# The second feed-forward's second layer as seven block products for eight, with a transposed output and a written task order

## The chip, the cores and the metric

The kernel runs on one core of one Trainium2 chip. The metric is device time of one execution in microseconds (us); smaller is better. Engines are named as the profile names them: PE (TensorE matmul), PEld (its weight load), DVE (VectorE), ACT (ScalarE), POOL (GpSimd), SP (SyncE, which here issues DMA transfers).

## What is computed

Masked attention over 4 batches and 8 heads (576 tokens, head size 64), then a gated feed-forward (512 to 1536 to 512), then a second feed-forward (512 to 2048 to 512) whose nonlinearity is h·cos(h). The change concerns the last lines.

```python
x = attention(q, k, v, tau)          # (4*576, 512), heads put side by side
gate = sigmoid(x @ w_gate)           # (2304, 1536)
x = (gate * (x @ w_val)) @ w_out     # (2304, 512)
h = x @ w_in                         # second feed-forward, first layer: (2304, 2048)
out = (h * cos(h)) @ w_out2          # second feed-forward, second layer: (2304, 512)
```

Every matmul operand is held as two parts of reduced precision ("hi" and "lo", lo being the operand minus hi), and one product is three matmuls: hi·hi, hi·lo, lo·hi.

## The kernel before

The 2304 tokens are handled as four blocks of 512 (the first 512 of each batch) and one small block of 256 (the last 64 of each batch). A class `Plan` (line 142) collects tasks, each with an engine, a cost and a due time, and `put_out` issues them: at each step the engine whose next task can begin first gets it, and among the tasks that can begin the one with the smallest due time goes first. Each engine then runs its tasks in exactly the order so fixed. For the attention (first `put_out`, line 919) the kinds of the tasks stand in a written list, `ORDER`; for everything behind it (second `put_out`, line 1453) the due times alone decide.

Behind the attention come two stages. In the **gated stage** (about 400 to 740 us) the first feed-forward runs; beside it `stage_weights` (line 991) reads the two 64-bit weight matrices of the second feed-forward, rounds them, splits them into hi and lo and stores them to a DRAM tensor `wd`: per slice of 256 columns the weights "i" (first layer), "s" (sums and differences of quarters of "i") and "z" (second layer). The lo parts are made on POOL (L987), the sums on DVE (L1019).

In the **second stage** (about 740 us to the end) the blocks go in two passes of two blocks, (0,1) and (2,3). For each of 8 slices of 256 hidden columns `quad` (line 1279) computes the first layer of both blocks at once as a 2x2 block product with seven block products instead of eight (42 matmuls for 48); its partial results are copied between PSUM banks by ACT (L1267) and added by DVE (L1270). Its inputs are seven "forms" of the activations (`forms_of`, line 1229). Then `cosine` works on each of four results: ACT scales to an integer (L1328), DVE removes the period in two steps (L1329 reads PSUM, L1331 reads SBUF alone), ACT takes the absolute value and the sine (L1333, L1334), DVE multiplies by h, which stands in PSUM (L1133), ACT takes the hi part (L1094), DVE the lo part (L1097). `second_c` (line 1343) is the second layer: per block, slice and half slice, four groups of 128 tokens as the stationary operand against 512 columns of "z", three matmuls each (L1360 to L1362); after every one or two slices the four PSUM banks are added by DVE to a running sum (L1370; the first time copied by ACT, L1368). That is 24 matmuls per block and slice, 384 for the two blocks of a pass. The small block runs in the first pass only (`U` its first layer, `S` its second). Weight slices of 1 MB come from `wd` by SP's queue into a ring of six (`fetch`, line 1421): three per slice and pass.

Of the kernel before, what the change touches and what calls it, by code (L numbers as in the profile page):

```python
# [19 lines left out]
P = 128  # L20
# [8 lines left out]
SM = 512  # L29
# [70 lines left out]

SHARED = (
# [19 lines left out]


# [19 lines left out]
class Plan:  # L142
# [31 lines left out]
    def task(self, engine, cost, key, fn, *needs, uses=(), moved=0.0, alone=False):  # L174
# [8 lines left out]
        return t  # L183

# [116 lines left out]
def tile_kernel(ctx: ExitStack, tc: tile.TileContext, q, k, v, tau, w_gate, w_val, w_out, w_in2, w_out2, out):  # L301
# [13 lines left out]
    minus_r = const.tile([P, P], F32R, tag="minus_r", name="minus_r")  # L315
    nc.vector.tensor_scalar(minus_r, ident, -1.0, None, op0=ALU.mult)
# [100 lines left out]
    at = tctx.enter_context(tc.tile_pool(name="at", bufs=1, side="right"))  # L417
    ps_s = psA.enter_context(tc.tile_pool(name="ps_s", bufs=2, space=PSUM))
# [509 lines left out]
    po = ctx.enter_context(tc.tile_pool(name="po", bufs=4, space=PSUM))  # L928
# [16 lines left out]
    END = len(items)  # L945

# [26 lines left out]

    for kd, ft in [("o", ft) for ft in range(NA)] + [(kd, ft) for ft in range(NA, NB) for kd in "gvo"]:
# [3 lines left out]
        loaded[kd, ft] = piece(plan, tmp, 2, kd, ft, wts[kd, ft], lambda i: first_use - 14.0 + i)  # L978

    wd = dpool.tile([P, NC, 3, 2, 1024], F32, name="wd")  # L980
    in_dram = {}

    def staged(key, hi, lo, needs, uses, to):
# [3 lines left out]
        last = task("POOL", 1.225, key, lambda: nc.gpsimd.tensor_tensor(st()[:, 1], lo(), f32(st()[:, 0]), op=ALU.subtract),  # L987
                    last, uses=[st, *uses])
        return task("SP", 0.47, key, lambda: nc.sync.dma_start(to, f32(st())), last, uses=[st], moved=1024)

    def stage_weights(ft, keys):

        done = {"i": [], "s": [], "z": []}
        ts = []
        for kd in "iz":
            for x, last, t in words(plan, tmp, 2, kd, ft, None, lambda i: next(keys)):
                i = x.i
                done[kd].append(staged(x.key, lambda x=x: f32(x.t), lambda x=x: f32(x.t), [last], [t],
                                       wd[:, ft, 0 if kd == "i" else 2, :, SM * i:SM * i + SM]))
                ts.append((x, last, t))  # L1000
            if kd == "i":
                (x0, l0, b0), (x1_, l1, b1) = ts
                key = next(keys)
                sf = ring("sf", [P, 4, 2, P], F32, 1)

                def quarter(x, f):
                    return f32(x.t).rearrange("p (c f n) -> p c f n", c=2, f=2)[:, :, f]

                def form(k):
                    return sf()[:, k]  # L1010
# [498 lines left out]
```

## Time and profile before

| | |
|---|---|
| median of 3 runs | 1134.39 us (1133.38 to 1135.61) |
| profiled execution, its own time | 1132.12 us |
| span of its profile, first to last instruction | 1130.0 us |
| PE busy | 1106.1 us (98%) |
| DVE / ACT / POOL busy | 875.2 (77%) / 730.4 (65%) / 408.9 us (36%) |
| granted TensorE clock, mean | 0.998 of full |

A matmul's row lasts longer than the distance to the next one, since matmuls are pipelined; the cost of one more or one less is the distance from start to start. The same holds, by a little, for DVE and ACT.

### The profile page before, as it was taken

The page shows a single profiled execution, that of the slowest core. Times are in us where ns is not written, and L with a number is a line of the kernel's source. Part 1 is how long each engine was busy: PE and PEld are TensorE (multiplying, and loading weights), DVE is VectorE, ACT ScalarE, POOL GpSimd, SP SyncE. Part 2 cuts the span into 40 slices and gives each one's busy share as a digit, 9 for nine tenths or more (in the row PEclk, how much of TensorE's full clock was granted, in tenths as well). Part 3 has the DMA queues.
Part 4 walks back from the last instruction along what each step waited for, and adds up shares of the span by engine and source line. Part 5 has one row for each costly group of instructions (what it writes and reads, how often), then busy time and mean ns, then how long its engine had stood idle before and what let it go on. Part 6 is the DMA issues. An engine that isn't in the chain of part 4 may idle for free. (4 is left out here: it accounts for less than half of the span.)

```text
span 1130.0 us, 17172 instructions
## 1 busy us (share of the span) xinstructions
PE 1106.1 (98%) x6031; PEld 950.5 (84%) x6031; DVE 875.2 (77%) x1620; ACT 730.4 (65%) x1409; POOL 408.9 (36%) x336
## 2 busy tenths in 40 slices
PE   7989999999999999999999999999999999999998
PEld 6878888888888888988888888878888888888887
DVE  6999989999998866787326889988576777857674
ACT  6889988897888855655314555477664645666461
POOL 3787788776778333451003555340000000000000
PEclk9999999999999999999999999999999999999999
DMA  6444544543244266595003988994343333735322
GB/s 172 137 122 150 149 135 119 183 136 94 74 132 152 82 229 217 168 359 178 22 1 105 338 319 317 350 321 151 112 142 106 125 112 116 275 122 182 143 75 75
DMA packets 64101, 183.57 MB, mean 162 GB/s; under 512 B 8336, under 2 KB 8592, under 8 KB 56080
## 3 DMA queue, kind: packets, MB, share of 16 engines
q1 hardware_dynamic: 63856, 182.15, 48.1%
q8 instruction: 48, 0.79, 0.3%
q10 hardware_dynamic: 160, 0.33, 0.1%
q14 instruction: 37, 0.30, 0.1%
HBM read 131.07 MB, written 51.38 MB: 161 GB/s over the span
## 5 line engine op out<-in xcount | busy, mean ns | idle before, releaser
L723 DVE SCALAR_TENSOR_TENSOR p<-s,sm,p 128x576 f32<-128x576 f32 x128 | 102.9, 813 | 9.6 <-ACT p L720 4.1
L715 DVE TENSOR_REDUCE sm<-s 128x1 f32<-128x576 f32 x144 | 105.6, 751 | 5.6 <-PE s L709 4.2
L1094 ACT ACTIVATE g<-g 128x512 fp32r<-128x512 f32 x118 | 74.0, 629 | 53.7 <-DVE g L1133 51.9
L1097 DVE TENSOR_TENSOR g<-g,g 128x512 fp32r<-128x512 f32 x118 | 94.9, 810 | 17.4 <-ACT g L1094 16.3
L1125 PE MATMUL h<-x,w 128*128 128x256 f32 (+1 forms) x304 | 101.3, 333 | 0.0
L1126 PE MATMUL h<-x,w 128*128 128x256 f32 (+1 forms) x304 | 101.3, 333 | 0.0
L1124 PE MATMUL h<-x,w 128*128 128x256 f32 (+1 forms) x304 | 101.3, 333 | 0.0
L1360 PE MATMUL o<-w,g 128*128 128x512 f32 x256 | 99.8, 390 | 0.0
L1361 PE MATMUL o<-w,g 128*128 128x512 f32 x256 | 99.7, 389 | 0.0
L1362 PE MATMUL o<-w,g 128*128 128x512 f32 x256 | 99.6, 389 | 0.0
L720 ACT ACTIVATE p<-s,sm 128x576 f32<-128x576 f32 x128 | 93.8, 747 | 8.6 <-DVE sm L715 5.3
L709 PE MATMUL s<-kk,qh 128*128 128x288 f32 x320 | 95.8, 318 | 1.3 <-DVE p L723 0.5
L686 POOL TENSOR_TENSOR PT<-praw,PT 128x512 fp32r<-128x512 f32 x60 | 78.3, 1306 | 48.6 <-ACT praw L681 24.4
L666 ACT ACTIVATE PT<-t 128x512 fp32r<-128x512 f32 (+1 forms) x160 | 85.9, 557 | 11.6 <-PE t L739 10.2
L709 PE MATMUL s<-kk,ql 128*128 128x288 f32 x320 | 88.9, 296 | 0.5 <-DVE ql L516 0.5
L368 POOL TENSOR_TENSOR w<-wt,w 128x512 fp32r<-128x512 f32 x30 | 41.2, 1381 | 126.9 <-ACT w L364 126.5
L739 PE MATMUL t<-ident,p 128*128 128x128 f32 x512 | 76.3, 274 | 4.9 <-DVE PT L677 1.9
L352 ACT ACTIVATE we<-wraw 128x512 f32<-128x512 f32 x68 | 45.6, 673 | 47.8 <-DMA wraw<-in_moe_w_out_dram 21.0
L1298 PE MATMUL h<-form,w 128*128 128x512 f32 x192 | 75.2, 392 | 1.1 <-ACT h L1267 1.0
L1300 PE MATMUL h<-form,w 128*128 128x512 f32 x192 | 74.7, 389 | 0.0
L1299 PE MATMUL h<-form,w 128*128 128x512 f32 x192 | 74.7, 389 | 0.0
L739 PEld LDWEIGHTS t<-ident,p 128*128 128x128 f32 x512 | 60.2, 140 | 15.1 <-DVE LT L677 3.0
(191 smaller groups left out, 3358.5 us busy)
## 6 DMA issues: line engine op xcount, KB each, us to landing
w<-wd SPq DMA_DIRECT2D x48, 1024.0 KB, 4.8
wd<-stage SPq DMA_DIRECT2D x48, 512.0 KB, 4.6
gd<-st SPq DMA_DIRECT2D x64, 256.0 KB, 3.6
wraw<-in_moe_w_out_dram SPq DMA_DIRECT2D x28, 512.0 KB, 5.2
raw_k<-in_k_dram SPq DMA_DIRECT2D x30, 304.0 KB, 4.7
raw_q<-in_q_dram SPq DMA_DIRECT2D x30, 288.0 KB, 4.5
wraw<-in_moe_w_in_dram SPq DMA_DIRECT2D x16, 512.0 KB, 5.3
early<-gd SPq DMA_DIRECT2D x7, 1024.0 KB, 6.5
```

What stands on the lines that cost most here:

```text
L709: nc.tensor.matmul(s[:, half, 0:HALF], qq[:, off:off + P], kk[:, k0:k0 + HALF], start=(i == 0), stop=(i == len(mms) - 1),)
L715: nc.vector.tensor_reduce(self.sm()[:, 0:1], self.s()[:, :, 0:HALF], axis=AX.XY, op=ALU.min)
L720: nc.scalar.activation(self.e, self.s()[:, :, 0:HALF], AF.Exp, bias=self.sm()[:, 0:1], scale=-1.0)
L723: nc.vector.scalar_tensor_tensor(self.e, self.s()[:, :, 0:HALF], self.sm()[:, 1:2], self.e, op0=ALU.is_le, op1=ALU.mult, accum_out=self.su ...
L739: nc.tensor.matmul(tp[:, c * P:(c + 1) * P], self.pn[:, k0:k0 + P], ident, is_transpose=True, start=(c == 0), stop=(c == 3))
L1097: nc.vector.tensor_tensor(g()[:, 1, 0:n], g32()[:, 0:n], f32(g()[:, 0, 0:n]), op=ALU.subtract)
L1124: nc.tensor.matmul(o, w_hi, x(0, c), start=begin, stop=False, **late)
L1125: nc.tensor.matmul(o, w_hi, x(1, c), start=False, stop=False, **late)
L1126: nc.tensor.matmul(o, w_lo, x(0, c), start=False, stop=c == KC - 1, **late)
L1360: nc.tensor.matmul(o(), hi, w_hi, start=i == 0, stop=False)
L1361: nc.tensor.matmul(o(), hi, w_lo, start=False, stop=False)
L1362: nc.tensor.matmul(o(), lo, w_hi, start=False, stop=i == len(parts) - 1)
```

## The change

The second layer of the two blocks of a pass is computed for slices 0 to 6 as a 2x2 block product with seven products for eight (`second_z`), after the scheme of `quad`. Block rows are the two halves of the slice's hidden columns, block columns the two token blocks. It needs seven forms of the hidden activations (`g_forms`: four subtractions in place, each of seven forms split into hi and lo) instead of four split results; a fourth set of staged weights, "t" (sums and differences of quarters of "z"); copies from PSUM bank to PSUM bank by ACT; and ten sums per slice into running sums `ys` and `y5`, of which `y5` is added at the end (`folded`). The weights are now the stationary operand and 512 tokens the moving one, so the running sums and the output stand transposed in DRAM, and the rows are put in order outside the kernel. Slice 7 of each pass is done as plain products, transposed too (`second_y`).

All tasks behind the attention have their place in a list, `LATER`: 668 numbers for PE, 779 for ACT, 852 for DVE, 218 for POOL, 234 for SP; a task's number is its place among its engine's tasks as the program makes them. For 430 operations with one result and two operands, `WHO` says whether DVE (D) or POOL (P) runs them: 194 are P. Before, these ran on DVE, other than the lo parts of staged weights and one of two additions in `from_a`, which ran on POOL. The staging of weights begins earlier (task 16 of the gated stage instead of the first task of its fourth slice). The sine of the second stage now waits for a table load that waits for every sigmoid, instead of the last one made.

```diff
+    def in_order(self, lines):
+        order = {e: [int(i) for i in line.split()] for e, line in lines.items()}
+        for e in order:
+            for i, t in enumerate(t for t in self.tasks if t.engine == e):
+                t.key = i
+        return order
...
+    def on_either(n, key, fn, *needs, uses):
+        if next(who) == "P":
+            return task("POOL", pool2(n), key, lambda: fn(nc.gpsimd), *needs, uses=uses)
+        return task("DVE", dve(n), key, lambda: fn(nc.vector), *needs, uses=uses, alone=True)
...
-    wd = dpool.tile([P, NC, 3, 2, 1024], F32, name="wd")
+    wd = dpool.tile([P, NC, 4, 2, 1024], F32, name="wd")
...
+        in_dram[ks, ft] = [staged(keys[2], src, src, needs, [sf], wd[:, ft, "iszt".index(ks), :, SM * i:SM * i + SM])
+                           for i, (src, needs, sf) in enumerate(sums_of(x0, x1, l0, l1, b0, b1, keys[2], view))]
+    begin = STAGED[0]
...
+        ft, (kd, ks, view) = i // 2, (("i", "s", "p (c f n) -> p c f n"), ("z", "t", "p (f c n) -> p c f n"))[i % 2]
...
-    G_ALL = [("g", 4), ("wraw", 2), ("stage", 3), ("sf", 1)]
+    G_ALL = [("g", 4), ("stage", 3)]
...
+    def halves(x, needs, at):
+        g = next_g()
+        last = task("ACT", act(SM, True), at, lambda: nc.scalar.activation(g()[:, 0], x(), AF.Copy), *needs, uses=[x, g])
+        return g, on_either(SM, at, lambda eng: eng.tensor_tensor(g()[:, 1], x(), f32(g()[:, 0]), op=ALU.subtract),
+                            last, uses=[x, g])
+    def g_forms(made, at):
...
+        f0 = halves(b11, [m11], at)
+        f5 = halves(b21, [m21], at)
+        f2 = halves(b22, [m22], at)
+        t1 = less(b11, b12, b11, m12, f0[1])
+        t3 = less(b12, b22, b12, m22, t1)
+        t2 = less(b22, b22, b11, t3, f2[1])
+        f3 = halves(b22, [t2], at)
+        f4 = halves(b12, [t3], at)
+        t4 = less(b21, b21, b22, t2, f5[1])
+        f6 = halves(b21, [t4], at)
+        f1 = halves(b11, [t1], at)
...
+    def second_z(p, q, forms, at):
...
+        def to_sum(ps, y, part, *needs):
+            if fresh:
+                t = task("ACT", act(SM), at - HOT, lambda: nc.scalar.activation(y()[:, part], ps(), AF.Copy), *needs, uses=[ps, y])
+            else:
+                t = task("DVE", dve(SM), at - HOT, lambda: nc.vector.tensor_tensor(y()[:, part], ps(), y()[:, part], op=ALU.add),
+                         *needs, uses=[ps, y])
...
+        for c in range(2):
+            x, y = o_bank(c), o_bank(2 + c)
+            p1 = product(x, plain(0, 0), 0, c, True)
+            k1 = moved(y, x, p1)
+            p2 = product(y, plain(1, 0), 5, c, False, k1)
+            to_sum(y, ys[a], c, p2)
+            p6 = product(x, mixed(1), 3, c, False, k1)
+            xs_.append((x, p6))
+        for c in range(2):
+            x, p6 = xs_[c]
+            y = o_bank(2 + c)
+            k2 = moved(y, x, p6)
+            p3 = product(y, mixed(3), 2, c, False, k2)
+            to_sum(y, ys[b], c, p3)
+            p7 = product(x, mixed(2), 4, c, False, k2)
+            e7 = to_sum(x, ys[b], 2 + c, p7)
+            p4 = product(x, plain(1, 1), 6, c, False, e7)
+            to_sum(x, ys[a], 2 + c, p4)
+        for c in range(2):
+            z = o_bank(2 + c)
+            p5 = product(z, mixed(0), 1, c, True)
+            to_sum(z, y5[c], slice(0, SM), p5)
...
+    def second_y(p, q, made, at):
+        done = folded(p, at - HOT)
+        for name, blk in zip("ba", PAIRS[p][::-1]):
...
+                    last = one_by_one[d] = task("PE", products(SM, 3), at, product, got, *one_by_one[d:d + 1] * f, *ready, uses=[o, w, g])
+                    if f == NF - 1:
+                        last = task("DVE", dve(SM), at - HOT, lambda o=o, y=y, d=d: nc.vector.tensor_tensor(
+                            y()[:, d], o(), y()[:, d], op=ALU.add), last, *(done if name == "b" else sums_last), uses=[o, y])
+                        r0 = blk * SM + d * P
+                        task("SP", 0.47, at, lambda r0=r0, y=y, d=d: nc.sync.dma_start(out[r0:r0 + P, :], y()[:, d]), last, uses=[y])
...
-    task("ACT", 1.4, END - 20.0, lambda: nc.scalar.activation(one, halfpi, AF.Sin), gates[0])
+    ready_sin = task("ACT", 1.4, END - 20.0, lambda: nc.scalar.activation(one, halfpi, AF.Sin), *gates)
...
-    plan.put_out()
+    plan.put_out(plan.in_order(LATER))
```

One `product` of `second_z` is three matmuls of 128x128 against 128x512 (w_hi·hi, w_hi·lo, w_lo·hi). The PE part of `LATER` mixes the products of `quad` for slice q+1 or q+2 with those of `second_z` for slice q, one or a few at a time.

## Rows read from the trace of the kernel before

**Rows 1.** The page's first lines: span, busy time of each engine.
```profile
span 1130.0 us, 17172 instructions
PE 1106.1 (98%) x6031; PEld 950.5 (84%) x6031; DVE 875.2 (77%) x1620; ACT 730.4 (65%) x1409; POOL 408.9 (36%) x336
```
**Rows 2.** The page's 40 slices: busy tenths of PE, and its granted clock.
```profile
PE   7989999999999999999999999999999999999998
...
PEclk9999999999999999999999999999999999999999
```
**Rows 3.** Windows: us, busy and count of PE, PEld, DVE, ACT, POOL, clock, DMA.
```profile
400.00:600.00 200.00, 200.00 (x1026) 171.77 (x1026) 122.48 (x171) 90.36 (x161) 54.41 (x37) 1.00 0.48 170
600.00:750.00 150.00, 148.14 (x720) 124.86 (x719) 129.86 (x183) 78.40 (x129) 68.48 (x48) 1.00 0.85 299
750.00:938.00 188.00, 187.92 (x906) 158.08 (x905) 137.52 (x209) 117.11 (x202) 4.28 (x3) 1.00 0.40 137
938.00:1126.00 188.00, 188.00 (x841) 155.83 (x840) 126.89 (x200) 104.01 (x182) 0.00 (x0) 1.00 0.39 138
```
**Rows 4.** Waits of PE from 400 us to the end, all that are listed.
```profile
PE h L1298 <- ACT h L1267: 1.0, 1, 1.0
PE h L1124 <- DVE g L1133: 0.9, 1, 0.9
```
**Rows 5.** Costliest groups, matmuls of the second layer: busy and mean ns of one.
```profile
L1360 PE MATMUL o<-w,g 128*128 128x512 f32 x256 | 99.8, 390 | 0.0
```
**Rows 6.** Timeline of PE at 1040 us, start and us; 36 matmuls apart.
```profile
1039.68 0.39 PE L1360 MATMUL o<-w,g 128*128 128x512 f32 x1
...
1047.84 0.39 PE L1360 MATMUL o<-w,g 128*128 128x512 f32 x1
```
**Rows 7.** Groups on DVE, window 600 to 750: two SBUF operands, then a PSUM operand.
```profile
L1097 DVE TENSOR_TENSOR g<-g,g 128x512 fp32r<-128x512 f32 x17 | 18.1, 1064 | 2.2 <-ACT g L1094 2.2
...
L1205 DVE TENSOR_TENSOR acc<-o,acc 128x512 f32<-128x512 f32 x30 | 20.4, 683 | 0.0
```
**Rows 8.** Groups on DVE, window 750 to 1130.
```profile
L1331 DVE SCALAR_TENSOR_TENSOR r<-ta,r 128x512 f32<-128x512 int32 x72 | 49.3, 687 | 1.1
...
L1097 DVE TENSOR_TENSOR g<-g,g 128x512 fp32r<-128x512 f32 x66 | 45.7, 696 | 7.2 <-ACT g L1094 6.2
```
**Rows 9.** Groups on POOL, 600 to 750: lo parts of staged weights.
```profile
L987 POOL TENSOR_TENSOR stage<-wt,stage 128x512 fp32r<-128x512 f32 x30 | 44.0, 1478 | 38.4 <-ACT stage L986 38.3
```
**Rows 10.** Timeline of DVE and ACT, start and us, back to back instructions.
```profile
1041.11 0.68 DVE L1097 TENSOR_TENSOR g<-g,g 128x512 fp32r<-128x512 f32 x1
1041.71 0.68 DVE L1329 SCALAR_TENSOR_TENSOR r<-ta,h 128x512 f32<-128x512 int32 x1
...
1040.37 0.63 ACT L1094 ACTIVATE g<-g 128x512 fp32r<-128x512 f32 x1
1040.89 0.63 ACT L1333 ACTIVATE r<-r 128x512 f32<-128x512 f32 x1
...
1059.68 0.58 ACT L1328 ACTIVATE ta<-h 128x512 int32<-128x512 f32 x1
1060.15 0.72 ACT L1334 ACTIVATE r<-r,halfpi 128x512 f32<-128x512 f32 x1
```
**Rows 11.** Timeline at 1049 us: a block product's last matmul, the ACT copy behind it.
```profile
1049.66 0.39 PE L1300 MATMUL h<-form,w 128*128 128x512 f32 x1
...
1050.08 0.58 ACT L1267 ACTIVATE h<-h 128x512 f32<-128x512 f32 x1 [3.07 <-PE h L1300]
```
**Rows 12.** Groups on DVE, window 600 to 750: sums of weight quarters.
```profile
L1019 DVE TENSOR_TENSOR sf<-wt 128x256 f32<-128x256 f32 x16 | 12.5, 780 | 0.0
```
**Rows 13.** DMA issues: KB each, median us from issue to landing.
```profile
w<-wd SPq DMA_DIRECT2D x48, 1024.0 KB, 4.8
```
**Rows 14.** Chain that ended last, its last two steps.
```profile
1125.98 0.24 PE o L1362
1126.24 0.69 DVE y L1370
```

More of the change, by code (lines that the diff above doesn't have):

```diff
@@ L99 @@
 ).replace(" ", "")
+FORMS = 2.0
+STAGED = (16.0, 9.0)
+LEAD = 14.0
+AHEAD = 8.0
+HOT = 5.0
+FETCH = 5.0
 SHARED = (
@@ L120 @@
 ).replace(" ", "")
+WHO = (
+    "DPPPPPDDPDDDDPDDDDDPPPDPDDDDDDDDDDPPDDDDDPDDPDDPDDPPDPDDPDPDDDDPDDDDPDDDPPDPPDDDDDDDDPDDDDDPPPPPPPPDPPDPDDPP"
+    "PPPDDDDPDDDDDPPDDPDPPDDPDDDDDPDDPPDDDDPDPDDDDDPDPDDPDDDDDDDDDDDDDDDDDDPDDDDDDDDDPDDDDDDDPDPDPPDDDDDPPPDDPDDP"
+    "DPPPPDDDPPPPPDDPPPDPDPPPDDPDPPDDDDPDPDDDDDPPDDPDDPPPDDPPDPDPPPPPPPDPPDDPPDPPPDDPDPPPPPDPPDPPDPPDDPPDPPDPDPPD"
+    "DPPDPDPDDDPPPDPDDDDPDDDDDPDPPPDDDPDDPDPDDPPPPDDDPPPDPPPPPDPPDPPPPPDPPPDDPPPPPDDDDPPPPPPPPDPDPPPPPPPPPDDDDD"
+)
+LATER = dict(
+    PE=(
[25 rows of a table added]
+    ),
+    ACT=(
[29 rows of a table added]
+    ),
+    DVE=(
[32 rows of a table added]
+    ),
+    POOL=(
[8 rows of a table added]
+    ),
+    SP=(
[8 rows of a table added]
+    ),
+)
 class Buf:
@@ L1035, in tile_kernel @@
+    begin = STAGED[0]
+    count = 2 * NC
+    step = (END - STAGED[1] - begin) / count
+    for i in range(count):
+        ft, (kd, ks, view) = i // 2, (("i", "s", "p (c f n) -> p c f n"), ("z", "t", "p (f c n) -> p c f n"))[i % 2]
+        mine = [begin + step * (i + k / 3) for k in range(3)]
+        jobs.append((mine[0] - AHEAD, lambda ft=ft, kd=kd, ks=ks, view=view, mine=mine: stage_weights(ft, kd, ks, view, mine)))
+    for _, job in sorted(jobs, key=lambda x: x[0]):
+        job()
     xs, x_done = {}, {}
@@ L1336, in cosine @@
         )
-        for engine, cost, fn, uses in steps:
-            last = task(engine, cost, at, fn, last, uses=uses, alone=engine == "DVE" and hh not in uses)
-        return multiply(n, at, hh, r2, last, g=g)
-    acc2 = {}
+        for i, (engine, cost, fn, uses) in enumerate(steps):
+            last = task(engine, cost, at, fn, last, ready_sin if i == 4 else None, uses=uses, alone=engine == "DVE" and hh not in uses)
+        if raw:
+            x = next_raw()
+            return x, task("DVE", dve(n), at, lambda: nc.vector.tensor_tensor(x(), hh(), r2(), op=ALU.mult), last, uses=[hh, r2, x])
@@ L1349, in second_c @@
         a = acc2[blk]
-        os = [out_bank() for _ in range(n // P)]
+        os, one_by_one = [out_bank() for _ in range(n // P)], [None] * (n // P)
+        sums = accs.setdefault(blk, [None] * (n // P))
         parts = [(ft, f) for ft in group for f in range(NF)]
```

273 lines of the change are left out of this document (167 added, 106 removed), and 102 rows, old and new, of tables (ACT, DVE, PE, POOL).

## The prediction

> **What bounds the kernel now.** I read the page's first lines, then its slices, then windows by stage, then the waits of PE. PE is busy for 98% of the span at full clock [rows 1, 2]. A busy PE need not be a full one, so the next view is the waits: from 400 us to the end only two stand there, 1.0 and 0.9 us, both at the change from the gated to the second stage [rows 4]. The timeline of PE shows why a mean of 390 ns [rows 5] is not the price of a matmul: 36 of them take from 1039.68 to 1047.84, which is 8.16/36 = 0.2267 us from start to start, with nothing left between [rows 6]. So behind 400 us the end is set by the number of matmuls and by nothing else. The other engines have room there: in the two windows from 750 to 1126, which are nearly the second stage, DVE is busy 137.5 + 126.9 = 264.4 of 376 us, ACT 117.1 + 104.0 = 221.1, POOL 4 [rows 3]. After the last matmul the chain needs one sum on DVE and one store [rows 14]; the change keeps both.
>
> **Part 1, the matmuls.** Before, the second layer of the four large blocks is 4 blocks x 8 slices x 2 halves x 4 groups x 3 = 768 matmuls (256 on each of three lines [rows 5]). After: 2 passes x 7 slices x 7 products x 2 column halves x 3 = 588, and slice 7 plain, 2 passes x 2 blocks x 2 x 4 x 3 = 96; together 684. All are 128x128 against 128x512 as before. 84 fewer at 0.2267 [rows 6] are **19.0 us** less on the engine that sets the end. The small block and the first layer keep their matmuls.
>
> **Part 2, what replaces them on ACT.** Each of 14 slices adds four copies between banks; the first sums are 10 a pass for 8; seven hi parts a slice for four give 14 x 3 = 42 more. One copy from PSUM takes 0.47 us from start to start, one from SBUF 0.52 [rows 10]: (56 + 4) x 0.47 + 42 x 0.52 = 50 us. ACT goes from 221 to 271 of the 376 - 19 = 357 us that PE would leave, 76%. I cost it at nothing, hidden behind PE; only the first slice of each pass is dense, where ACT takes all ten sums.
>
> **Part 3, what replaces them on DVE and POOL.** Sums: a slice now has ten, so 6 x 10 + 8 = 68 a pass on DVE for 28, together +80. Lo parts: 7 x 7 + 4 = 53 a pass for 32, +42. Subtractions in place: 4 x 7 x 2 = 56. `folded`: 8. Of the 189 operations of this stage for which `WHO` chooses (these lo parts, subtractions and folds, the small block's lo parts, the second pass's forms), I count 108 P. DVE therefore gets 80 + 42 + 56 + 8 - 108 = +78. It now has 209 + 200 = 409 instructions [rows 3] at 0.60 from start to start [rows 10], about 245 us; +78 makes 292 of 357 us, 82%. POOL gets 108 x 1.48 [rows 9] = 160 us, 45%.
>
> That sum leaves out that the two disturb each other. In the window from 600 to 750, where POOL is busy 68.5 of 150 us (46%), a DVE subtraction with both operands in SBUF takes 1064 ns [rows 7]; in the second stage, with POOL idle, the same line takes 696 [rows 8]. So one waits 0.37 us on average at the share of POOL that the change would bring. An operation of DVE with an operand in PSUM takes 683 ns in that same window [rows 7], so it does not wait. Of the second kind are the sums, the first step of the cosine and the multiplication; of the first kind the 72 second steps of the cosine (L1331) and the 189 - 108 = 81 choices left on DVE: 153 x 0.37 = 57 us. DVE is then at 349 of 357 us. Without any wait it is at 82%, with the waits of the window before at 98%: it comes within reach of PE. The Trainium skill, "Perfetto Trace Analysis", section "Optimizing Scalar/DVE Operations", says that moving operations between DVE and GpSimd might not help, since GpSimd's only port is DVE's second. If it gave nothing here, DVE would keep 108 x 0.60 = 65 us more than the 292 and stand at 357 of 357; the row with the PSUM operand speaks for more room than that.
>
> What PE loses by it the trace of before doesn't show, so I bound it. From below: the windows from 938 to 1126 show no loss at all [rows 3], so 0. From above: if DVE waits a quarter more than in the window, 153 x 0.46 = 70, it stands at 362, and with some 10 us at the beginnings and ends of the two passes, in which it waits for PE, the excess over 357 is 15. I take **5 us**, nearer to the lower end, since the stretch from 600 to 750 had DVE busy 129.9 of 150 (87%) beside POOL at 46% and PE lost only those two waits [rows 3, 4].
>
> **Part 4, the chain inside a slice.** The products of one slice hang together through four banks: product, copy on ACT, next product into the same bank. Rows show the round trip: the last matmul of a product of `quad` begins at 1049.66, the next matmul could begin at 1049.89, the copy runs from 1050.08 for 0.58 [rows 11], so a product that needs it can begin some 0.8 us after PE could have gone on. Other work must lie between. I read the PE list of `LATER` against the order in which the tasks are made: between such a pair there are nearly everywhere two products of `second_z` or one of `quad`, 6 x 0.2267 = 1.36 us or more; in one place there is one product, 0.68. So the chain costs 0.1 us as long as ACT and DVE take these copies and sums at once; if they stand behind one other instruction, 0.5 to 0.6 us, it still fits. What goes beyond is in the 5 us.
>
> **Part 5, staging and transfers.** The set "t" adds for 8 slices four sums of 256 columns at up to 0.78 [rows 12] and two lo parts at up to 1.06 [rows 7], 8 x 5.2 = 42 us, if all is on DVE, to 252 of 350 us in the windows from 400 to 750 [rows 3]: hidden, 84%. ACT gets 16 copies, 10 us to 169. Staging now begins earlier, so the crowd of DMA before 750 (share 0.85 [rows 3]) thins out. The two waits of rows 4 lie just there; I take **1 us** of gain for them (from 0 to 1.9). In the second stage 14 more loads of 1 MB come, four a slice for three, over 14 x 25 us; a load lands in 4.8 us [rows 13]. A ring slot is free at the earliest after the last product of its slice, which by the list is 12 us of PE work ahead of its next use. DMA share is 0.4 now [rows 3] and rises to 0.55: hidden. SP issues in order, so a load whose slot is late holds back those behind it; with 12 us against some 7 for two loads that is covered, and without the cover a late load costs a wait of a few us per slice.
>
> **Part 6, the ends.** The last plain products need the last cosines. By the list 14 us of PE work lie between the product that feeds the first of them and its use; the chain is nine steps of 0.5 to 0.7 us with a POOL step of 1.5, some 8 us. Nothing added. The single table load ahead of the sines waits for all sigmoids; first sines come after the last gated product's gate, nothing added. The attention keeps its order: nothing.
>
> **Sum.** -19.0 - 1 + 5 = -15.0 us. Against the profiled execution's own 1132.12 that is 1117.1 (span 1115); against the median, 2.3 us above it, **1119.3 us**.
>
> **The rivals.**
> *PE stays the bound* (forecast): 1114 with no new loss and both old waits gone (-19.0 - 1.9 + 0.5), 1123 with 9 us of new loss. For it: DVE at 87% with POOL at 46% cost PE nothing to speak of; against it: the chain of part 4 hangs on DVE and ACT more tightly than the gated stage did.
> *DVE with POOL becomes the bound of both passes*: DVE needs 362 to 372 us for 357, new loss 9 to 16: 1123 to 1131, at its middle 1127. For it the 98% above; against it that many of the waits of rows 7 came from operations that were issued behind the same ACT copy, which need not meet here.
> *The waits grow until it is slower than before*. Same place, other size: to be 2.3 us slower, DVE must need 357 + 19 + 2.3 + 1 = 379 us, so (379 - 292)/153 = 0.57 us of wait for each operation with two SBUF operands; that is the point from which it decides. At 0.65 it needs 391, and the time is 1119.3 - 5 + 34 = 1148 us. Against it: 0.37 is measured. For it: a POOL operation takes 1.48 us [rows 9], and a wait can be as long. The Trainium skill, "SBUF — State Buffer", section "Who interferes with whom", calls this an exclusive lock and not a sharing of bandwidth; the two durations of rows 7 and 8 agree in kind, and a wait of a whole operation each time would be 153 x 1.48 = 226 us.
> *The saving is given back elsewhere*: the gated stage, whose order changes too and in which PE has no slack to win, loses PE time to late weights or late forms, 9 to 18 us more than the forecast: 1128 to 1137. For it: 350 us of full PE [rows 3] can only get worse; against it: every engine beside PE has room there.
>
> **How the numbers follow.** Forecast 0.66, DVE the bound 0.20, slower by waits 0.07, given back 0.07 (0.04 of it still faster, 0.03 within 0.2%). Faster: 0.66 + 0.20 + 0.04 = 0.90; within 0.2% (2.3 us, about what a measurement of this kernel can tell from no change) 0.03; slower 0.07. The range goes from 1114, the forecast's low end, to 1128, which takes in some two thirds of the second case and leaves out 0.07 + 0.06 + 0.07.
>
> **What the profile after would show.** The matmuls of the second layer number 684 at 0.227 us from start to start. Right: PE's waits behind 400 us sum to 3 to 8 us, spread over the second stage, released by DVE sums or ACT copies; DVE there is busy over 85%, its lo parts at 0.9 to 1.1 us; POOL near 45%. Wrong: waits of PE in the gated stage, waits on loads of weights, or DVE busy without a gap and PE waiting at each slice.

## The result, and the profile after

The median after is 1123.11 us (1119.40 to 1124.61, 4 runs) against 1135.0 (1133.38 to 1137.15, 4 runs) before on the same chip: a ratio of 0.989, 95% interval 0.986 to 0.992. It is faster by 1.1%, which is little but clear of no change by the interval. The time lies inside the range, 3.8 us above the forecast of 1119.3. The two profiled executions lie closer together than the medians, 1124.61 against 1132.12 us, since that of after is the highest of its four and that of before lies below all of its four.

The page's first lines, to be held against [rows 1]:
```profile
span 1122.5 us, 17476 instructions
PE 1090.5 (97%) x5947; PEld 936.4 (83%) x5947; DVE 919.5 (82%) x1722; ACT 783.7 (70%) x1527; POOL 575.3 (51%) x468
```
PE has 5947 matmuls for 6031, the 84 fewer. The windows by stage, columns as in [rows 3], the last one shorter because the span is:
```profile
400.00:600.00 200.00, 195.20 (x995) 166.77 (x994) 148.42 (x228) 108.11 (x197) 65.06 (x54) 0.99 0.80 280
600.00:750.00 150.00, 150.00 (x722) 126.75 (x721) 96.32 (x148) 61.43 (x103) 68.35 (x51) 1.00 0.60 201
750.00:938.00 188.00, 187.89 (x927) 159.47 (x926) 157.19 (x244) 142.42 (x257) 80.10 (x58) 1.00 0.51 177
938.00:1118.00 180.00, 175.74 (x767) 142.92 (x765) 160.29 (x246) 131.29 (x234) 80.44 (x58) 1.00 0.53 189
```
Here the reader sees two things that [rows 3] did not have. The first window, full before, lacks 4.8 us of PE. The last one lacks 4.3, but most of that is its end: the last matmul begins at 1114.84 and the window goes to 1118. In between, with POOL at 80 us and DVE at 157 and 160 us a window, PE is as full as it was.

The waits of PE from 400 us on, for [rows 4]:
```profile
PE h L1276 <- ACT ta L1294: 2.8, 1, 2.8
PE o L539 <- ACT g L1246: 1.7, 1, 1.7
PE h L1460 <- DVE form L1402: 0.8, 1, 0.8
PE o L1669 <- DVE y L1646: 0.3, 1, 0.3
PE o L540 <- DVE g L1249: 0.2, 1, 0.2
PE o L1579 <- DVE y L1589: 0.2, 1, 0.2
```
The two waits of before are gone. In their place stand two larger ones, both on ACT and both of the gated stage (L1276 is a gated product, L1294 its sigmoid's gate, L539 the plain product's first matmul, L1246 the hi part it reads).

**Where the time went.** Busy time hides small gaps, so I added up, from the trace of PE, by how much the distance between the starts of two matmuls exceeds 0.2267 us (0.120 for one of 256 columns). I call that PE's loss; it holds gaps as well as matmuls that ran at a lower clock. For the profiled pair it closes the account:

| term | forecast | measured |
|---|---|---|
| 84 matmuls fewer, at 0.2267 | -19.0 | -19.0 |
| PE's loss, 775 us to the last matmul (0.45 before, 3.65 after) | +5 (0 to 15) | +3.2 |
| PE's loss at the change of stage, 725 to 775 us (3.0, 0.5) | -1 (-1.9 to 0) | -2.5 |
| PE's loss at the beginning of the gated stage, 400 to 450 us (0.3, 7.5) | 0 | +7.2 |
| from the last matmul's end to the span's end (3.9, 7.5) | 0 | +3.6 |
| the rest | | +0.1 |
| sum | -15.0 | -7.5 |

The middle of the kernel gives -18.3, better than forecast. The two ends take back 10.8 us, which the prediction had put at nothing. How much the beginning takes differs from one execution to the next: in the six other profiled executions with the same order up to there (below: the unaltered kernel again, the one with the end of SP's list rearranged, and the four that alter the second stage and keep the lists) PE lost 2.8 to 5.5 us from 400 to 450 us, and 3.8 to 7.7 us from 400 to 725 us, where this one lost 7.7. So this profile is at the high end. It lies 1.5 us over its kernel's median, and that of before 2.9 us under its own, which is the way from -7.5 to the medians' -11.9.

### The profile page after: what moved, and what is told of

Read it like the earlier page. It is cut to its first block, busy times and chain, and to the rows that moved or that the text cites. A ratio compares the mean times of both kernels' runs of the same rounds, so it can differ in the third digit from the quotient of the medians.

```text
span 1122.5 us, 17476 instructions
## 1 busy us (share of the span) xinstructions
PE 1090.5 (97%) x5947; PEld 936.4 (83%) x5947; DVE 919.5 (82%) x1722; ACT 783.7 (70%) x1527; POOL 575.3 (51%) x468
## 4 chain that ended last, share of the span: by engine, by line
PE 84%; DVE 5%; ACT 4%; DMA 3%; issue 2%; POOL 1%; SPq 0%; DVEq 0%; ACTq 0%; POOLq 0%
PE h L1277 6%; PE h L1278 6%; PE h L1276 6%; PE s L847 6%; PE t L877 5%; PE o L540 5%; PE o L539 5%; PE o L541 5%; PE h L1459 4%; PE h L1460 4%; PE h L1461 4%; PE o L1579 4%; PE o L1580 4%; PE o L1581 4%; PE v L938 3%; PE v L937 3%
## 5 line engine op out<-in xcount | busy, mean ns | idle before, releaser
L1505 POOL TENSOR_TENSOR g<-raws,g 128x512 fp32r<-128x512 f32 x68 | 91.8, 1359 | 107.0 <-ACT g L1504 80.4
L1276 PE MATMUL h<-x,w 128*128 128x256 f32 (+1 forms) x304 | 101.3, 333 | 0.0
L804 ACT ACTIVATE PT<-t 128x512 fp32r<-128x512 f32 (+1 forms) x160 | 85.8, 557 | 12.5 <-PE t L877 11.0
L1589 DVE TENSOR_TENSOR y<-o,y 128x512 f32<-128x512 f32 x120 | 78.6, 684 | 10.7 <-PE o L1581 10.4
L488 ACT ACTIVATE we<-wraw 128x512 f32<-128x512 f32 x68 | 45.1, 668 | 49.8 <-DMA wraw<-in_moe_w_out_dram 20.6
L1513 POOL TENSOR_TENSOR raws<-raws 128x512 f32<-128x512 f32 x30 | 42.6, 1422 | 69.9 <-DVE g L1505 34.0
L1579 PE MATMUL o<-g,w 128*128 128x512 f32 x196 | 76.9, 392 | 0.2 <-DVE y L1589 0.2
L1580 PE MATMUL o<-g,w 128*128 128x512 f32 x196 | 76.4, 390 | 0.0
L1581 PE MATMUL o<-g,w 128*128 128x512 f32 x196 | 76.4, 390 | 0.0
L1460 PE MATMUL h<-form,w 128*128 128x512 f32 x192 | 75.0, 390 | 0.8 <-DVE form L1402 0.8
```

Of the source, the lines that this page charges most:

```text
L1276: nc.tensor.matmul(o, w_hi, x(0, c), start=begin, stop=False, **late)
L1460: nc.tensor.matmul(ps(), of(0, c), lo, start=False, stop=False, skip_group_check=True)
L1579: nc.tensor.matmul(ps(), of(0, c), hi, start=begin, stop=False, skip_group_check=True)
L1580: nc.tensor.matmul(ps(), of(0, c), lo, start=False, stop=False, skip_group_check=True)
L1581: nc.tensor.matmul(ps(), of(1, c), hi, start=False, stop=True, skip_group_check=True)
```

## The experiments

In kernels in which a list was written anew, line numbers stand one higher than in the trace of after, with the needless matmuls five; where lines of code were taken out, those behind them stand that much lower. Four kernels ran once each: the second by due times, and those with less work for DVE, for PE and for both. What is said of them rests on their traces, since the unaltered kernel's own times lie up to 6 us apart.

**The written order against due times.** Is the gain that of the seven products, or does it need the written lists? The first kernel has everything of the change but the order:
```diff
-    plan.put_out(plan.in_order(LATER))
+    plan.put_out()
```


> The changed kernel without its written list: the tasks behind the attention are ordered by their due times, as in the kernel before; seven products, the operations on POOL and the transposed output stay. It parts the seven products from the order. Theory 2 (84 matmuls less are worth 19 us only if the order keeps PE fed): PE loses 10 to 25 us in the second stage, 1120 to 1135 us. Rival (the order adds nothing, the saving is the products' alone): PE loses no more than in the changed kernel, and without the waits at 413 us the time is 1112 to 1118 us. On the lock between DVE and POOL: with due times alone, DVE's lo parts in the second stage take 0.9 to 1.1 us, as between 600 and 750 us before (1.06), where the written list has them at 0.74.

It took 1157.08 us (1155.57 to 1158.37), ratio to before 1.020 [1.016, 1.023]: slower than the kernel before by 23 us and than after by 34, and beyond the 1120 to 1135 us that the theory had given. With 84 matmuls fewer, the change under these due times is a loss. The other half, the eight products of before under a written list, was not run; but PE's loss before from 400 us on is 3.9 us in all (0.3, 0.1, 3.0 and 0.45 by stretch), so no order alone could have won the 11.9 us. The windows of the second stage show the holes in PE that the lists keep out:
```profile
750.00:938.00 188.00, 186.68 (x892) 154.86 (x892) 159.04 (x230) 137.00 (x242) 74.65 (x50) 1.00 0.46 158
938.00:1155.00 217.00, 191.73 (x785) 148.53 (x783) 179.26 (x251) 132.89 (x236) 82.27 (x58) 0.95 0.44 162
```
PE's loss behind 775 us is 42.7 us for 3.65. Some 6 to 7 us of it are not gaps: 34 matmuls there stand about 0.43 us apart for 0.2267, and the granted clock of the last window is 0.95. The same choice of engines stands in both kernels, so the groups on DVE show what an order does to the DVE and POOL collisions. First the kernel after, then this one (second step of the cosine, and the lo part; both read SBUF alone; the number behind the comma is the mean in ns):
```profile
L1537 DVE SCALAR_TENSOR_TENSOR r<-ta,r 128x512 f32<-128x512 int32 x72 | 52.7, 735 | 0.9
L1505 DVE TENSOR_TENSOR g<-raws,g 128x512 fp32r<-128x512 f32 x38 | 27.9, 741 | 4.9 <-ACT g L1504 4.9
```
```profile
L1538 DVE SCALAR_TENSOR_TENSOR r<-ta,r 128x512 f32<-128x512 int32 x72 | 61.0, 858 | 0.7
L1506 DVE TENSOR_TENSOR g<-raws,g 128x512 fp32r<-128x512 f32 x38 | 37.6, 1001 | 7.0 <-ACT g L1505 6.8
```
With POOL idle these were 687 and 696 [rows 8]. By the lists an operation takes 0.05 us more, by due times 0.17 and 0.31; the lo part's 1001 ns is in the 0.9 to 1.1 us that was expected of due times.

Do those waits cause the 34 us, or the order itself? The second kernel takes POOL out of the second stage as well: the last 189 letters of `WHO` all D, under due times.

> Due times in place of the written list, and DVE alone in the second stage (POOL does none of its 108 operations). With POOL the kernel of due times took 1157 us, its DVE waiting 0.17 to 0.32 us per operation with two SBUF operands for POOL. If these waits are why due times lose 35 us, this kernel is no slower than 1160 us though DVE has 65 us more to do; if it is the order itself, it is at 1170 to 1190 us.

It took 1165.51 us, between what the two theories had given, so it doesn't part them cleanly. It has no POOL work to collide with, but 108 x 0.60 = 65 us more on DVE, and is 8 us slower; under the lists (below) the same move costs 28 us. By the difference the collisions may hold up to 20 of the 34 us, and some 14 are the order's own; that is an estimate from one run, and the collisions' share is not shown. Of the 8 us, 5.7 were lost from 450 to 725 us, where POOL's work is the same in both; behind 775 us PE lost 44.6 us, against 42.7 with POOL. The longest waits of PE behind 700 us are the same in kind in both, here those of the first and then of the second kernel:
```profile
PE h L1460 <- DVE raws L1548: 6.1, 2, 3.2
PE h L1460 <- ACT h L1429: 5.7, 3, 2.6
PE o L540 <- ACT g L1505: 4.0, 1, 4.0
```
```profile
PE h L1460 <- DVE raws L1548: 13.4, 7, 3.1
PE o L540 <- ACT g L1505: 6.0, 1, 6.0
PE h L1460 <- ACT h L1429: 4.9, 3, 3.1
```
`quad` (L1460) waits for the cosine's multiplication (L1548) to free its banks and for its own copies (L1429): a chain of the kind of part 4, in an order that puts other work ahead of it.

**How near DVE is to the end.** The prediction's second rival had DVE with POOL as the bound. Three kernels move the two sides apart. The first gives POOL's 108 operations of the second stage to DVE, in the place that they had in planned time.

> The 108 operations that POOL has in the second stage go to DVE, put into its list where they stood in time; the other lists stay. What it tells is what POOL is worth. By counts DVE then has 595 instructions at 0.60 us, 357 us and 5 us of wider ones, and nothing to wait for on POOL: as long as PE's own 357. If POOL's operations come at almost no cost to DVE (0.05 us each): the kernel with DVE alone is bound by DVE, 15 to 40 us slower than the control, 1135 to 1165 us. Rival (what POOL takes over is given back in waits for the common port): within 8 us of the control.

It took 1151.41 us (1148.99 to 1152.23), 1.016 [1.013, 1.019] of before; the unaltered kernel beside it, 1123.53. POOL is worth 28 us, for 65 us of work in DVE's time, inside the 15 to 40 us that were expected of a POOL that costs DVE little. The windows have DVE at 92% and 96% and PE with holes, and the longest wait is a product of `second_z` (L1580) for the sum that frees its bank:
```profile
750.00:938.00 188.00, 184.35 (x880) 151.67 (x879) 172.27 (x280) 134.97 (x246) 6.32 (x6) 1.00 0.50 174
938.00:1142.00 204.00, 188.89 (x797) 144.62 (x795) 195.61 (x314) 137.03 (x242) 0.00 (x0) 1.00 0.47 166
```
```profile
PE o L1580 <- DVE y L1590: 9.2, 14, 1.6
```
The same two groups on DVE as above, under the same lists but with POOL idle, stand at 684 and 683 ns for 735 and 741, which gives the 0.05 us a second time:
```profile
L1506 DVE TENSOR_TENSOR g<-raws,g 128x512 fp32r<-128x512 f32 x106 | 71.6, 683 | 6.9 <-ACT g L1505 6.6
L1538 DVE SCALAR_TENSOR_TENSOR r<-ta,r 128x512 f32<-128x512 int32 x72 | 49.0, 684 | 0.8
```
The second kernel takes load off DVE instead: the second of DVE's two steps of the cosine (L1537, 72 operations; counted from ACT's scaling it is the third step) is left out, and the absolute value reads the result of the step before.
```diff
-            ("DVE", dve(n), lambda: nc.vector.scalar_tensor_tensor(
-                r2()[:, 0:n], ki()[:, 0:n].bitcast(I32), -C2, r()[:, 0:n], op0=ALU.mult, op1=ALU.add), [ki, r, r2]),
-            ("ACT", act(n, True), lambda: nc.scalar.activation(r2()[:, 0:n], r2()[:, 0:n], AF.Abs), [r2]),
+            ("ACT", act(n, True), lambda: nc.scalar.activation(r2()[:, 0:n], r()[:, 0:n], AF.Abs), [r, r2]),
```


> The changed kernel without the third step of the cosine (the 72 operations with two SBUF operands on DVE, some 0.6 to 0.73 us each, 43 to 53 us of DVE); the absolute value reads the second step's result, so the period is removed a little less exactly. All else and the other lists stay. Theory (behind 450 us PE holds the changed kernel, DVE only just does not): no gain outside the run's scatter, PE's loss behind 775 us from 3.65 to 2 to 3.6 us. Rival (DVE already holds it): that loss goes and the time falls by more than 4 us.

It took 1123.13 us in its one run, no gain. Some 43 us less on DVE (72 at 0.60) took PE's loss behind 775 us from 3.6 to 3.2 us. DVE has 133 and 141 us in these windows, and PE is no fuller than it was:
```profile
750.00:938.00 188.00, 187.87 (x927) 159.48 (x926) 133.11 (x207) 142.85 (x258) 77.24 (x57) 1.00 0.52 179
938.00:1116.00 178.00, 174.49 (x762) 142.15 (x760) 140.99 (x211) 128.97 (x232) 76.97 (x58) 1.00 0.53 188
```
So in the kernel after PE holds the end, as forecast. The third kernel asks how much less PE work would still shorten it: one of the three matmuls of each product of `second_z` is left out, 196 x 0.2267 = 44.4 us.
```diff
-                nc.tensor.matmul(ps(), of(0, c), lo, start=False, stop=False, skip_group_check=True)
-                nc.tensor.matmul(ps(), of(1, c), hi, start=False, stop=True, skip_group_check=True)
+                nc.tensor.matmul(ps(), of(0, c), lo, start=False, stop=True, skip_group_check=True)
```


> The third matmul (weights' lo part times hi part) of each product of second_z is left out: 14 x 14 = 196 matmuls less, 44.4 us of PE, all other work and the lists as in the changed kernel; its output lacks that term. The step of the prediction that puts DVE at 349 of 357 us says that DVE then holds the second stage: the time falls by no more than 8 to 12 us. Rival (operations on DVE wait for POOL by 0.05 us here, not 0.37, so DVE needs some 300 us): it falls by 25 to 44 us, short of 44 where PE's list now finds its copies and sums too late.

It took 1108.37 us. PE's loss behind 775 us is 34.3 us, so of 44.4 us taken from PE 30.7 came back and 13.7 stayed. That lies between the two theories, 8 to 12 and 25 to 44. The prediction's sum had DVE at 349 of 357 us, 8 us of room; that the room under these lists is near this is no proof of the sum, because what PE waits for is not DVE first. The longest two waits:
```profile
PE o L1580 <- ACT o L1595: 5.2, 14, 0.7
PE o L1580 <- DVE y L1589: 2.8, 6, 0.6
```
L1595 is the copy from bank to bank of part 4. A product of two matmuls covers 0.45 us of that round trip and not 0.68, so the missing matmul also took cover from the chain. The last of these kernels makes both edits.

> Both cuts: the 196 third matmuls of second_z are left out (44.4 us of PE) and the third step of the cosine too (43 to 53 us of DVE). With the first cut alone the span was 1106.3 us and PE lost 34.3 us behind 775 us. If DVE's load was what held that kernel, the loss falls to 5 to 20 us and the span to 1075 to 1092 us. If it was the chains of the products within a slice (copy on ACT, sum on DVE, in a list made for a slower PE), whatever DVE's load, the loss stays over 25 us and the span over 1097.

It took 1099.81 us, PE's loss there 21.8, again between what the two theories had given (5 to 20, over 25). Of the 30.7 us that came back, 12.5 hung on DVE's load; the rest stayed with DVE at 78% and 83%. Whether that rest is the copies' chain alone, this run can't tell: the lists were written for other durations.

**The end.** In the kernel after the last matmul starts at 1114.84 and the span ends at 1122.5. The timeline of SP's queue and of DVE and PE at the end:
```profile
1112.59 1.80 SPq L1649 DMA_DIRECT2D out_dram<-y  x4
1114.43 0.56 SPq L1685 DMA_DIRECT2D out_dram<-y  x1
1115.31 3.79 SPq L1649 DMA_DIRECT2D out_dram<-y  x6
```
```profile
1113.91 2.05 DVE L1646 TENSOR_TENSOR y<-o,y 128x512 f32<-128x512 f32 x3 [1.35 <-PE o L541]
```
```profile
1114.84 0.39 PE L541 MATMUL o<-g,w 128*128 128x512 f32 x1
```
The last sum is done at 1115.96, 6.5 us before the span's end. SP issues eleven stores within 6.5 us, among them one of the small block (L1685) and two of the first pass, whose data had been there for long. SP's list has them between the last stores. Its first store there belongs to a sum that comes late, and SP stands before it while sums behind it are done (waits of SP's queue from 1000 us on):
```profile
SPq L1649 <- DVE y L1646: 26.5, 2, 26.2
```
The experiment moves the three old stores (187, 191, 194) ahead of SP's last weight loads and puts the last eight in the order in which their sums come:
```diff
-  ... 225 231 228 229 187 194 233 191 232 227 226 230
+  ... 225 227 226 228 229 231 230 233 232
```


> The changed kernel with the end of SP's list reordered: three stores of the first pass that stand at its end go to 1050 us, the eight last stores stand in the order in which DVE makes their sums. Theory: the changed kernel ends 7.4 us after its last matmul because eleven stores of 256 KB go out in one row behind a store that waits for a late sum; with this the end comes about 4 us after the last matmul, as in the kernel before (3.8), so 3 to 3.5 us less in all. Rival (the last sums or the transposed stores themselves are slower): the end stays 6 to 7.4 us behind the last matmul.

It took 1120.04 us (1118.26 to 1120.75), 0.987 [0.985, 0.990] of before. The first pass's stores now go out at 1067 us, the last row has eight stores instead of eleven and is issued from 1108.58 on:
```profile
1066.89 1.45 SPq L1650 DMA_DIRECT2D out_dram<-y  x2
1068.39 0.80 SPq L1686 DMA_DIRECT2D out_dram<-y  x1
1069.28 16.12 SPq L1723 DMA_DIRECT2D w<-wd  x4
1108.58 6.88 SPq L1650 DMA_DIRECT2D out_dram<-y  x8
```
From the last matmul's end to the span's end it is 4.0 us for 7.5 (before: 3.9): 3.5 of the account's +3.6. The trace shows this; the medians, 1120.04 against 1123.11, have ratios to before whose intervals overlap.

**The beginning of the gated stage.** ACT's timeline of the kernel after shows what the two waits of 2.8 and 1.7 us hang on:
```profile
412.87 0.69 ACT L488 ACTIVATE we<-wraw 128x512 f32<-128x512 f32 x1 [5.96 <-DMA r<-xd]
415.54 0.69 ACT L488 ACTIVATE we<-wraw 128x512 f32<-128x512 f32 x1 [1.98 <-DMA wraw<-in_moe_w_out_dram]
416.11 0.60 ACT L1294 ACTIVATE ta<-h 128x512 f32<-128x512 f32 x1
...
422.53 0.66 ACT L488 ACTIVATE we<-wraw 128x512 f32<-128x512 f32 x1 [2.81 <-DMA wraw<-in_moe_w_out_dram]
423.09 0.58 ACT L1294 ACTIVATE ta<-h 128x512 f32<-128x512 f32 x1
423.57 0.62 ACT L1246 ACTIVATE g<-g 128x512 fp32r<-128x512 f32 x1
```
By its list ACT converts weights (L488) before it takes the sigmoid (L1294), and the weights are on their way. Theory one: the place of these conversions in ACT's list is the cause, and moving the sigmoid ahead ends the wait. Theory two: the loads are the cause, and the wait goes elsewhere.
```diff
-  "ACT": 0 2 160 145 1 4 144 3 6 164 161 ...
+  "ACT": 0 160 2 145 1 4 144 3 161 164 6 ...
```


> The changed kernel with the first eleven entries of ACT's list reordered: the two sigmoids and the first hi part of the gated stage go ahead of the weight conversions that wait for loads; nothing else changes. Theory 1 (ACT's written order makes PE wait at 413 to 425 us): the waits of 2.8, 1.7 and 0.2 us there go, and with them the lower clock behind them, so PE's loss from 400 to 450 us falls from 7.5 to under 1.5 us and the span from 1122.5 to about 1116. Rival (the loads of the weights are late whatever stands ahead of them): the first product with the output weights waits instead, and the loss stays at 5 us or more.

It took 1120.23 us (1118.47 to 1124.12), 0.988 [0.985, 0.992] of before; PE's loss from 400 to 450 us is 3.5 us, from 450 to 725 it is 1.6. The wait on the sigmoid did go; in its place stand others, of 0.9, 0.4 and 0.2 us on DVE and POOL and 0.2 on ACT, and the loss is neither under the 1.5 of theory one nor at the 5 of theory two. The next kernel brings the loads forward on SP instead (`0 120 121 1` becomes `0 1 120 121`).

> The changed kernel with the second weight load of the gated stage issued ahead of the two small-block loads on SP, ACT's list untouched. Theory 1: the second weight conversion on ACT begins about 2 us earlier (413.5 for 415.5), the first wait of PE falls from 2.8 to 0.5 to 1 us, the second (1.7 us, for the fourth load) stays: loss from 400 to 450 us 3 to 6 us. Rival (loads, not ACT's list): both waits go, loss under 1.5 us.

It took 1120.86 us (1119.46 to 1121.79), 0.988 [0.985, 0.991]; loss 2.8 us. ACT's second conversion begins at 412.88 for 415.54, and the wait on the sigmoid is 1.1 us. Neither could be judged without knowing what the beginning does by itself, so the kernel after was run again, unaltered.

> The changed kernel once more, unaltered, beside the next ones on the same chip. All theories: 1119 to 1125 us, 7.4 us from the last matmul to the end. Theory 1 says that the waits of PE between 410 and 430 us depend on when the first weight loads land and so differ from run to run: loss from 400 to 450 us between 2.5 and 8 us. Rival (they are fixed by the order alone): 7.5 us again.

It took 1123.53 us (1119.91 to 1125.73), 0.991 [0.988, 0.995] of before. Its own loss from 400 to 450 us is 3.0 us, with one wait on the sigmoid:
```profile
PE h L1277 <- ACT ta L1295: 2.2, 1, 2.2
```
So the 7.5 of the first profile is the high end of a scatter, and from it the two edits can't be told: from 400 to 725 us they lose 5.1 and 3.6 us, the unaltered order 3.8 to 7.7. Their medians are 2 to 3 us under after's, with ratios to before whose intervals overlap. Theory one falls as the whole story. What does not go away by reordering was tried the other way round: if the loads behind the attention set the pace of the first 20 us, PE can idle there at no cost. The kernel puts 24 needless matmuls, 24 x 0.2267 = 5.4 us, ahead of the stage's first product.
```diff
+    idle = ph.tile([P, 512], F32, tag="h3", name="idle")
+    for _ in range(24):
+        nc.tensor.matmul(idle, xs_a[:, 0, 0, 0:P], xs_a[:, 0, 0], start=True, stop=True)
```


> The changed kernel with 24 idle matmuls (24 x 0.2267 = 5.4 us) on PE ahead of the gated stage; their result is read by nobody, all else and the lists are unaltered. Theory (the lists of the gated stage are made for a PE that comes later than it does, and the weight loads behind the attention's last store set the pace of its first 20 us): the idle matmuls fill a time in which PE would wait, PE's waits from 400 to 450 us fall from 2.2 to 4.8 us to under 1 us, and the last matmul of PE comes no more than 1 to 3 us later than in the control (1110.5), 1120 to 1126 us. Rival (the loads and the work on ACT wait for PE's products, so that all of it moves along): the same waits stand behind the idle matmuls, and the time is 5 us above the control, 1127 to 1130 us.

It took 1122.36 us (1121.13 to 1124.69), 0.989 [0.986, 0.993] of before: 5.4 us of PE time that cost nothing that can be measured. No wait of PE from 400 to 470 us is left, and the loss from 400 to 725 us is 0.5; with the 5.4 us of needless work that is 5.9, in the midst of the 3.8 to 7.7 of the unaltered order. So something other than PE sets the pace there. That it is the loads is what ACT's timeline says; no run made the loads themselves faster. The windows from 400 to 450 us, of the kernel after, of the unaltered one run again, and of this one:
```profile
400.00:450.00 50.00, 45.20 (x198) 36.75 (x197) 26.38 (x42) 23.12 (x43) 16.05 (x15) 0.97 0.72 252
```
```profile
400.00:450.00 50.00, 47.78 (x230) 39.75 (x230) 30.31 (x44) 23.07 (x43) 19.54 (x17) 1.00 0.75 269
```
```profile
400.00:450.00 50.00, 50.00 (x235) 41.93 (x234) 29.55 (x44) 22.30 (x41) 18.88 (x17) 1.00 0.74 265
```
PE is full, and its last matmul ends at 1111.7 us against 1110.5 in the unaltered kernel. The lists fit a PE that comes 5 us later than it does. In the kernel after PE's first gated product starts at 405.59 us and SP's first load of `w_out` is issued at 408.95, behind the attention's last store. Before, with this stage ordered by due times, the loss was 0.3 us. By due times the same tasks as after (the first kernel of these experiments) lose 0.3 us here too: SP issues the first two of these loads together at 407.66, and ACT has both converted before its sigmoid at 413.83:
```profile
411.37 0.68 ACT L489 ACTIVATE we<-wraw 128x512 f32<-128x512 f32 x1 [5.76 <-DMA wraw<-in_moe_w_out_dram]
412.43 0.67 ACT L489 ACTIVATE we<-wraw 128x512 f32<-128x512 f32 x1 [0.38 <-DMA wraw<-in_moe_w_out_dram]
```
But it loses 7.0 us from 450 to 725 us, so its gated stage is no better in sum; an order of these tasks that keeps PE full in the whole stage was not found.

**All edits at the ends together**, and two products exchanged in PE's first five (`6 0 1 12 7` becomes `6 0 1 7 12`):

> All reorderings of the lists together: ACT's head, SP's head, SP's end, and on PE the second value product of the first block ahead of the first product that needs a bank back; no instruction is added or taken away. Theory 1 with the end's theory: loss from 400 to 450 us under 1 us, 4 us from the last matmul to the end, waits of the second stage unchanged at 3.5 us: 1112 to 1115 us, 7 to 10 us less than the control. Rival (what is won at the head is given back between 450 and 600 us, since the weights that now come later are waited for there): 1116 to 1120 us.

It took 1117.60 us (1115.37 to 1120.22, 6 runs), 0.987 [0.984, 0.990] of before, and 5.9 us less than the unaltered kernel beside it. It beats the kernel before; against the kernel after, five of its six runs lie below the lowest of the four beside it. The time falls in the rival's range, 1116 to 1120, and not in the theory's, but not for the rival's reason: from 450 to 725 us the loss is 0.9 for 0.8. In the profiled executions of the two, 3.5 of 3.6 us are the end, and the loss from 400 to 450 us is 2.6 for 3.0; the other 2 us of the medians I can't place.

## Why the prediction was right, point by point

**Is it luck?** In part. The mechanism held: PE sets the end, and 84 matmuls at their start-to-start distance are what the change saves. But the time stayed in the range with errors of both signs: the middle gave 3.3 us more than forecast, and the ends took 10.8 that stood at nothing. By the profiled pair alone, -7.5 from the median of 1134.4, it would be 1126.9 us, near the upper end of the range. Of the signs named beforehand, the 684 matmuls, the sum of PE's waits (6.0 us, forecast 3 to 8), DVE at 86% in the second stage and POOL at 44% came. The lo parts at 0.9 to 1.1 us did not come, nor did waits spread over the second stage: 4.7 of the 6.0 us stand in the gated stage, which the prediction had named as a sign of being wrong.

**Part 1 was right to the tenth.** The second layer has 684 matmuls, and -19.0 us of the account is theirs. The mean duration of a matmul's row is still 390 to 392 ns, and would have promised 33.

**Part 2 was right.** ACT is busy 142.4 + 131.3 = 273.7 us behind 750, forecast 271, and none of the waits of PE listed there is put down to it (the small ones that the list leaves out are in part 4).

**Part 3 had the right counts and one mis-sized term.** DVE runs 244 + 246 = 490 instructions there, forecast 487; POOL is busy 160.5 us, forecast 160. But the wait of an operation with two SBUF operands, taken as 0.37 us from the gated stage [rows 7], is 0.05. For 153 operations that is 8 us and not 57, and by start-to-start distances DVE stands at 300 of 357, not at 349 (by its rows, which overlap a little, it is busy 157.2 + 160.3 = 317.5 us). The row was read rightly and carried to a place where the order was another: under due times the same operations wait 0.17 and 0.31 us, near the row. What an operation waits is thus a matter of order: 741 against 1001 ns for the same work. The Trainium skill, "SBUF — State Buffer", section "Who interferes with whom", speaks of an exclusive lock; the two figures agree in kind, but means alone don't show a lock. The Trainium skill, "Perfetto Trace Analysis", section "Optimizing Scalar/DVE Operations", warns that moving operations between these two might not help; here it helped, and the 108 operations on POOL are worth 28 us.

**The 5 us of new loss came out as 3.2**, most of it at the change of passes and in the last slice: 1.1 us before a form of the second pass (whose lo part on DVE takes 1.8 us a piece), 0.6 at the small block, 0.4 at the last plain products and 1.2 in the bank chain. It was taken as DVE's crowding; but taking 72 operations off DVE took 0.4 us of it. That the value was near is luck; its reason was not right.

**Part 4 was right in kind.** The list of waits has 0.2 us for the bank chain, forecast 0.1; by start-to-start distances PE loses 1.2 us in four places where a product of `second_z` comes late, three behind the copy L1595 and one behind the sum L1589. The prediction had put such an excess into the 5 us. The written order is what keeps it there, as the kernel by due times shows; and with one matmul less in each product the copies' waits come up at once.

**Part 5 failed for the beginning.** The two waits of [rows 4] did go, and with them 2.5 us, more than the 1.9 that they were listed with. But the step took the room that DVE and ACT have in the gated stage as a whole ("hidden, 84%") as if it held in its first 20 us. There room counted for nothing: in the trace ACT stands before a conversion whose weights have not landed, and 5.4 us of added PE work cost nothing. The fourth rival, the saving given back in the gated stage, is thus half true: its place and its "late weights" are right, its size of 9 to 18 us beyond the forecast is not; by 450 us 2.5 to 7.2 us more than before were lost, by 725 us 3.4 to 7.3. Why the same order loses 3.8 us in one execution and 7.7 in another stays open.

**Part 6 failed for the end.** "Nothing added" was argued from the chain of the last cosines, and that held. What it left out is the order of the stores on SP, which stood in the same list. It is 3.6 us, and the experiment gave it back.

**The rivals.** PE stays the bound of the second stage: right, by the kernel with less DVE work. DVE with POOL as the bound: not here, though with some 14 us less PE work the next limit, the chains and DVE together, would have come. Its price was not worked out from its own sum: 362 to 372 us for 357 is an excess of 5 to 15, not a new loss of 9 to 16. Slower than before by waits: the waits never came near 0.57 us; but slower than before is just what the change is without its lists.

## What to carry to other kernels

Count the saving at the start-to-start distance, then read the two ends of the order by themselves: what each queue has in its last ten tasks, and which loads the first twenty microseconds wait for; that is where part of this saving went. A mean wait between two engines belongs to the order in which it was measured; carry it as a range from nothing to that row. Where a transformation trades one engine's work for chains between three, the order of tasks is part of its price: here the same instructions gave 1123 and 1157 us.

## What the runs showed of the hardware

The two waits at the beginning cost more than their own 4.5 us. In the kernel after the granted clock falls behind them:
```profile
410.00:420.00 10.00, 7.17 (x32) 5.63 (x31) 3.17 (x6) 4.19 (x8) 1.49 (x2) 1.00 0.84 271
420.00:430.00 10.00, 8.03 (x28) 5.92 (x27) 2.92 (x5) 3.85 (x7) 2.49 (x3) 0.83 0.77 276
```
From 426.15 to 429.14 us seven matmuls stand 0.43 us apart for 0.2267, the lower of the two levels (1.2 for 2.4 GHz), after PE had been idle for 2.8 and 1.7 us; that is 1.4 us more. In the unaltered kernel run again, with one such wait of 2.2 us, the clock from 400 to 450 us is 1.00 and no matmul is slow. The size of the waits alone does not settle it: with POOL's work on DVE, one wait of 2.6 us was followed by seven slow matmuls (granted clock 0.83 from 410 to 420 us), and with less work on DVE, waits of 2.6 and 1.1 us were followed by none.

The end of the kernel after moved 2.88 MB in one row at 360 to 395 GB/s, so each store of 256 KB in that last row costs about 0.7 us. Which of the beginnings an execution gets, 2.8 or 7.5 us of loss by 450 us under the same lists, I could not settle.
